# Decode block with sliding-window attention and a feed-forward: the loads' buffers as one tile, and three weight matrices in two loads each

## The chip, the cores and the metric

The kernel runs on one core of a Trainium2 chip, as one launch. The metric is the device time of one execution in microseconds (us), given as the median of several runs. The profile is of one execution taken by the hardware profiler. Engines: TensorE (PE, with PEld for its weight loads), VectorE (DVE), ScalarE (ACT), GpSimd (POOL) and SyncE (SP), which issues every DMA of this kernel.

## The reference

All values are float32. B = 2 tokens, D = 512, 32 query heads over 8 key/value heads of 128, a window of the last 4096 positions of a cache of 32768, and a feed-forward of F = 1792.

```python
mod = silu(c) @ w_mod                       # [2, 6*512]: sa, ca, ga, sb, cb, gb
h = layernorm(x) * (1 + ca) + sa
q = h @ wq                                  # [2, 32*128]
o = softmax(q . k_window / sqrt(128)) @ v_window
x = x + ga * (o @ wo)
h = layernorm(x) * (1 + cb) + sb
x = x + gb * (silu(h @ w1) @ w2)
```

Bytes read: w_mod 6.3 MB, wq 8.4 MB, keys and values 67.1 MB, wo 8.4 MB, w1 and w2 3.7 MB each.

## The kernel before

All weights, keys and values stream through a ring of 8 buffers of 16 KB per partition (pool `ring`, L55; `stream`, L69). Each load takes the next buffer, so load number i can be issued when the work that reads load i - 8 is done. SP issues the loads in one order: w_mod in 4 loads of 128 rows (`load_rows`, L72), then wq in 4 (L112), then by `fetch` (L324) keys and values of the 8 heads and 2 tokens, 32 loads of 2 MB, then wo in 4 loads of 8 rows per partition (`load_runs`, L91, called at L473), w1 in 3 and w2 in 5. In `load_rows` partition p holds row 128k + p of load k; in `load_runs` partition p holds neighbouring rows of the matrix, one contiguous run.

The two tokens lie on few partitions. A vector of 512 is held in one of two ways: the "ch" form (c_ch, x_ch; L100, four DMAs with runs of 128 bytes, L105 to L110) fits contraction in blocks of 128 rows, and the "spread" form (x_sp, L474, one DMA with runs of 512 bytes) puts 128 neighbouring values on one partition. `turned` (L268) transposes a spread tile so that partition p, column k is element 4p + k.

Steps: c is transposed (cT, L235), silu is taken, and w_mod gives m_ch (sa, ca in "ch" form, L246) and m_sp (the other four, spread, L249). Layernorm a (`moments`, L209) and mod_ch give h_a, transposed to hq_T (L263). Then 64 instructions for q (L285) and a rearrangement to qbd.

The loop over heads (L448) is software-pipelined: `keys` transposes K on VectorE (kT, L337), `scores` on TensorE (L349), `maxima`, `exponentials` on ScalarE, `turn` and `weighted` (o, L423) for the head before. `inorder` keeps the program's order on an engine.

After the last head come the sums and the normalised output oTn (oq L512, L515). Output projection: for q = 0 to 23 a matmul of 512 columns with rows of wo (acc_o, L550), four column groups in turn; for q = 24 to 31 four matmuls of 128 columns each (ao, L561); `gather` (L519) copies acc_o on ScalarE and folds it into ao with four matmuls after q = 27. `busy(n)` (L534) runs n matmuls on a junk tile whose result is not used (L537): busy(5) after q = 15 and after q = 23, busy(2) after the last. A float32 matmul is two instructions in the trace.

Then aoT (L572), x1T, the mean (L582), hT_b, and w1's matmuls (hid, L595) for k = 0 to 3, with the variance (L606) after k = 1 and busy(2) after k = 2. hidT (L615), silu, uT (L627), w2's matmuls: tt = 0 to 7 wide (acc_yw, L631), tt = 8 to 13 in four pieces (acc_y, L643) with a gather after tt = 10, then yo (L653, L654) and the store (L656).

```python
    for q in range(24):
        g = q % 4
        inorder(nc.tensor.matmul(acc[32 * g : 32 * g + 32, :], oTn[:, q, :],
            wot[q // 8][:, q % 8, :], start=(q < 4), stop=(q >= 20)))
        if q in (15, 23):
            busy(5)
```

Of the kernel before, what the change touches and what calls it, by code (L numbers as in the profile page):

```python
# [23 lines left out]
def adaln_block(  # L24
# [23 lines left out]

    head = ctx.enter_context(tc.tile_pool(name="head", bufs=1))
    id4 = head.tile([P, 32], F32, name="id4")
    ring = ctx.enter_context(tc.tile_pool(name="ring", bufs=RING))  # L55
# [7 lines left out]
    def const(shape, name):  # L63
        return consts.tile(shape, F32, name=name)

    def bank(tag, name):
        return (psum1 if tag in "CO" else psum).tile([P, 512], F32, tag=tag, name=name)

    def stream(name):  # L69
        return ring.tile([P, 4096], F32, tag="st", name=name)  # L70

    def load_rows(name, w, k, width):  # L72
        t = stream(f"{name}{k}")[:, :width]
        nc.sync.dma_start(t, w[k * P : (k + 1) * P, :])
        return t

    def load_k(b, h):
        t = stream(f"k{h}_{b}")
        nc.sync.dma_start(
            t, k_cache[b, h, SK - W :, :].rearrange("(p n) d -> p (n d)", p=P)  # L80
        )
        return t

    def load_v(b, h):
        t = stream(f"v{h}_{b}")
        nc.sync.dma_start(
            t, v_cache[b, h, SK - W :, :].rearrange("(p n) d -> p (n d)", p=P)
        )
        return t

    def load_runs(name, w, per, lo, hi):  # L91

        e = w.shape[1]
        t = stream(f"{name}{lo}")[:, : (hi - lo) * e].rearrange("p (q e) -> p q e", e=e)
        nc.sync.dma_start(t, w.rearrange("(p q) e -> p q e", q=per)[:, lo:hi, :])
        return t


    x2 = x.rearrange("b s d -> (b s) d")
    x_sp, x_ch, c_ch = const([P, P], "x_sp"), const([P, P], "x_ch"), const([P, P], "c_ch")  # L100
    for t in (c_ch, x_ch, x_sp):
        nc.vector.memset(t, 0.0)
    wm = [load_rows("wm", w_mod, 0, 6 * D)]
    rows8 = lambda t: t.rearrange("(ab r) m -> ab r m", r=16)[:, 0, :]
    for t, src in ((c_ch, c), (x_ch, x2)):  # L105
        for b in range(B):
            nc.sync.dma_start(
                rows8(t)[b : 2 * 4 : 2, :].rearrange("a (k c) -> a k c", k=4),
                src[b, :].rearrange("(k a c) -> a k c", k=4, a=4),
            )  # L110
    wm += [load_rows("wm", w_mod, k, 6 * D) for k in range(1, 4)]
    wqt = [load_rows("wq", wq, k, HQ * DH) for k in range(4)]  # L112
# [80 lines left out]

    oTn = const([P, 32, 32], "oTn")
    nc.gpsimd.memset(oTn, 0.0)
    mod_ch = const([P, 2, P], "mod_ch")
    mod_sp = const([P, 4, P], "mod_sp")
    x1 = const([P, P], "x1")

# [31 lines left out]
        return mean, rstd  # L231


    cT = const([P, 4, 32], "cT")
    nc.vector.transpose(cT.rearrange("p k r -> p (k r)"), c_ch)  # L235
    sg = silu_exp(cT, "sgc", [P, 4, 32])
    scT = const([P, 4, 32], "scT")
    nc.vector.tensor_mul(scT, cT, sg)
    m_ch = bank("A", "m_ch")[:, : 2 * P]
    m_sp = bank("D", "m_sp")  # L240
    for k in range(4):
        ab = wm[k][:, : 2 * D].rearrange("p (s k a c) -> p a s k c", s=2, k=4, a=4)
        cd = wm[k][:, 2 * D :].rearrange("p (s g m) -> p g s m", s=4, g=4)
        for g in range(4):
            r = slice(32 * g, 32 * g + 32)
            nc.tensor.matmul(m_ch[r, :], scT[:, k, :], ab[:, g], start=(k == 0), stop=(k == 3))  # L246
        for g in range(4):
            r = slice(32 * g, 32 * g + 32)
            nc.tensor.matmul(m_sp[r, :], scT[:, k, :], cd[:, g], start=(k == 0), stop=(k == 3))  # L249
        if k == 0:  # L250
            mean_a, rstd_a = moments(x_ch, "a")
            xn = once.tile([P, P], F32, tag="xp", name="xn_a")
            nc.vector.tensor_scalar(
                xn, x_ch, mean_a, rstd_a, op0=ALU.subtract, op1=ALU.mult
            )

    nc.vector.tensor_copy(mod_ch[:, 0, :], m_ch[:, :P])
    nc.vector.tensor_scalar(mod_ch[:, 1, :], m_ch[:, P:], 1.0, None, op0=ALU.add)
    h_a = once.tile([P, P], F32, tag="pr", name="h_a")
    nc.vector.tensor_mul(h_a, xn, mod_ch[:, 1, :])  # L260
    nc.vector.tensor_add(h_a, h_a, mod_ch[:, 0, :])
# [6 lines left out]
    def turned(t, name):  # L268
        o = const([P, 4, 32], name)
        nc.vector.transpose(o, t.rearrange("p (m k) -> p k m", k=4))  # L270
        return o
# [9 lines left out]
    for k in range(4):  # L281
        wv = wqt[k].rearrange("p (n s g m) -> p n g s m", n=2, s=4, g=G)
        for n in range(2):
            for g in range(G):
# [4 lines left out]
                    start=(k == 0),  # L289
                    stop=(k == 3),  # L290
                )
    for n in range(2):
        qT = once.tile([P, D], F32, tag="wide", name=f"qT{n}").rearrange("p (s j r) -> p s j r", s=4, r=32)
        nc.vector.transpose(qT.rearrange("p s j r -> p (s j r)"), q_ps[n])  # L294
        for g in range(G):
            r = slice(32 * g, 32 * g + 32)
# [8 lines left out]
        for i in range(4):  # L305
            r = slice(32 * i, 32 * i + 32)
# [14 lines left out]
    kt, vt, wot, kT = {}, {}, [], {}  # L321
# [173 lines left out]
    for r in (0, 64):  # L495
# [4 lines left out]
            start=True,  # L500
            stop=True,
# [32 lines left out]
    def busy(n):  # L534

        for _ in range(n):
            inorder(nc.tensor.matmul(  # L537
                junk[0:32, :256],
                id4,
                selh.rearrange("p m y -> p (m y)")[:, :256],  # L540
                start=True,
                stop=True,
            ))
# [4 lines left out]
    for q in range(24):  # L548
        g = q % 4
        inorder(nc.tensor.matmul(  # L550
            acc[32 * g : 32 * g + 32, :],
            oTn[:, q, :],
            wot[q // 8][:, q % 8, :],
            start=(q < 4),
            stop=(q >= 20),
        ))
        if q in (15, 23):
            busy(5)
    for q in range(24, 32):
        for g in range(4):  # L560
            inorder(nc.tensor.matmul(  # L561
                ao[32 * g : 32 * g + 32, :],
                oTn[:, q, :],
                wot[3][:, q - 24, g * P : (g + 1) * P],
                start=(q == 24),
                stop=(q == 31),
            ))
# [4 lines left out]
    nc.vector.transpose(aoT, ao.rearrange("p (m k) -> p k m", k=4))  # L572
    x1T = once.tile([P, 4, B], F32, tag="x1T", name="x1T")
# [19 lines left out]
    for k in range(4):  # L593
        for g in range(4):
            inorder(nc.tensor.matmul(  # L595
                hp[32 * g : 32 * g + 32, :],
                hT[:, k, :],
                w1t[k][:, g * FC : (g + 1) * FC],
                start=(k == 0),
                stop=(k == 3),  # L600
            ))
# [15 lines left out]
    for b in range(B):  # L617
# [5 lines left out]
            op0=ALU.mult,  # L623
            op1=ALU.add,
# [4 lines left out]
    for tt in range(WIDE):  # L629
        g = tt % 4  # L630
# [4 lines left out]
            start=(tt < 4),  # L635
            stop=(tt >= WIDE - 4),
# [4 lines left out]
    for tt in range(WIDE, T2):  # L641
        for g in range(4):
# [4 lines left out]
                start=(tt == WIDE),  # L647
                stop=(tt == T2 - 1),
# [35 lines left out]
```

## Time and profile before

| | before |
|---|---|
| median of 3 runs | 236.98 us (236.98 to 237.25) |
| the profiled execution | 236.89 us |
| its span, first to last instruction | 235.0 us |
| mean granted TensorE clock | 0.869 |
| PE / PEld / DVE / ACT / POOL busy | 146.5 / 45.9 / 114.6 / 25.4 / 10.3 us |
| moved by DMA | 97.69 MB, mean 416 GB/s |

The span is the time from the first to the last instruction; the execution's time has a little more around it. Busy times of engines overlap. The slices of the page cut the span in 40 equal parts; a digit is a busy share in tenths. PEclk is the share of TensorE's full clock that was granted. In a timeline row stand the start, the time, the engine, the line, the operation, what it writes and reads, the number of instructions and, in brackets, the idle time of the engine before them with what ended it.

### The profile page before, as it was taken

How to read it: one execution, taken by the hardware profiler on the slowest of the kernel's cores; microseconds unless marked ns; L12 is line 12 of the kernel's file. 1: busy time of each engine (PE TensorE's matmuls, PEld its weight loads, DVE VectorE, ACT ScalarE, POOL GpSimd, SP SyncE). 2: the span in 40 equal slices, each digit the busy share in tenths (PEclk: the TensorE clock that was granted, in tenths of full speed). 3: DMA queues.
4: the chain of work that ended last, by engine and by line, in shares of the span. 5: the costliest groups of instructions: out<-in, count | busy, mean ns of one | idle time of the engine just before them, and what ended most of it. 6: DMA issues, size and time to landing. Idle time of an engine off the chain costs nothing.

```text
span 235.0 us, 2644 instructions
## 1 busy us (share of the span) xinstructions
PE 146.5 (62%) x1094; PEld 45.9 (20%) x1094; DVE 114.6 (49%) x176; ACT 25.4 (11%) x56; POOL 10.3 (4%) x30
## 2 busy tenths in 40 slices
PE   0086546367187577667549519626743967788993
PEld 0032101101011121121112102111211222335332
DVE  0634000793694792693892792595298050002130
ACT  2200000100300200200200200200020021003210
POOL 8600000100000000000000000000000000000000
PEclk9999975759869997999976967965985799999999
DMA  6999999999999999999999999999999999999991
GB/s 253 426 438 427 427 438 427 424 439 427 429 441 424 427 438 427 429 438 424 429 435 429 427 432 432 432 429 432 428 429 429 429 432 429 432 426 422 421 412 56
DMA packets 7603, 97.69 MB, mean 416 GB/s; under 512 B 920, under 2 KB 936, under 8 KB 1576
## 3 DMA queue, kind: packets, MB, share of 16 engines
q1 hardware_dynamic: 7592, 97.54, 97.5%
q8 instruction: 8, 0.13, 0.2%
q14 instruction: 3, 0.02, 0.0%
HBM read 97.53 MB, written 0.00 MB: 415 GB/s over the span
## 4 chain that ended last, share of the span: by engine, by line
DMA 64%; DVE 22%; PE 10%; ACT 2%; issue 1%; SPq 1%; DVEq 0%
DVE kT L337 16%; DMA wo<-in_A_wo_dram 14%; DMA k<-in_A_k_cache_dram 14%; DMA v<-in_A_v_cache_dram 13%; DMA wq<-in_A_wq_dram 13%; DMA w<-in_B_w_dram 7%; PE s L349 5%; DMA wm<-in_w_mod_dram 3%; DVE zp L395 2%; PE o L423 2%; PE q L285 1%; DVE xp L393 1%; ACT pr L381 1%; DVE mx L359 1%; ACT L381 1%
## 5 line engine op out<-in xcount | busy, mean ns | idle before, releaser
L337 DVE STREAM_TRANSPOSE kT<-k 128x1024 f32<-128x1024 f32 x64 | 73.7, 1210 | 1.6 <-DMA k<-in_A_k_cache_dram 1.6
L349 PE MATMUL s<-kT,qbd 128*32 128x512 f32 x256 | 44.5, 670 | 11.2 <-DVE kT L337 11.1
L423 PE MATMUL o<-v,ptb 128*32 128x512 f32 x256 | 38.5, 730 | 19.8 <-DMA v<-in_A_v_cache_dram 19.3
L359 DVE TENSOR_REDUCE mx<-s 128x1 f32<-128x512 f32 x8 | 5.5, 691 | 40.1 <-PE s L349 40.1
L349 PEld LDWEIGHTS s<-kT,qbd 128*32 128x32 f32 x256 | 11.1, 126 | 45.8 <-issue 24.1
L285 PE MATMUL q<-wq,hq_T 128*32 128x512 f32 x64 | 11.2, 836 | 10.1 <-DMA wq<-in_A_wq_dram 10.1
L423 PEld LDWEIGHTS o<-v,ptb 128*32 128x32 f32 x256 | 8.1, 124 | 35.8 <-issue 33.1
L402 PE MATMUL pT<-zp,id 128*32 128x256 f32 x64 | 5.6, 418 | 13.9 <-DVE zp L395 13.9
L379 ACT COPY bias<-bp 128x1 f32<-128x1 f32 x8 | 1.3, 159 | 111.9 <-PE bp L377 111.9
L537 PE MATMUL junk<-selh,id 128*32 128x256 f32 x46 | 11.3, 380 | 0.0
L294 DVE STREAM_TRANSPOSE qT<-q 128x512 f32<-128x512 f32 x2 | 1.4, 718 | 18.6 <-PE q L285 18.3
L395 DVE TENSOR_TENSOR zp<-xp,group 128x1024 f32<-128x1024 f32 x8 | 9.8, 1225 | 0.2
L393 DVE STREAM_TRANSPOSE xp<-pr 128x512 f32<-128x512 f32 x8 | 5.6, 701 | 4.4 <-ACT pr L381 4.4
L217 PE MATMUL mean_a<-mv_a,avg 128*128 128x1 f32 x2 | 0.6, 362 | 10.6 <-DVE mv_a L214 10.6
L361 PE MATMUL mT<-ident,mx 128*1 128x128 f32 x16 | 3.0, 270 | 6.4 <-DVE mx L359 6.4
L550 PE MATMUL acc_o<-wo,oTn 128*32 128x512 f32 x48 | 5.8, 598 | 1.9 <-DMA wo<-in_A_wo_dram 1.6
L537 PEld LDWEIGHTS junk<-selh,id 128*32 128x32 f32 x46 | 5.0, 110 | 6.7 <-issue 3.5
L438 PE MATMUL o_all<-ob,selh 128*64 128x128 f32 x64 | 5.7, 304 | 0.8 <-ACT ob L432 0.8
L270 DVE STREAM_TRANSPOSE xT<-x_sp 128x128 f32<-128x128 f32 x1 | 0.4, 403 | 11.8 <-DMA x_sp<-in_A_x_dram 11.8
L432 ACT COPY ob<-o 128x512 f32<-128x512 f32 x8 | 4.7, 585 | 10.3 <-PE o L423 10.3
L285 PEld LDWEIGHTS q<-wq,hq_T 128*32 128x32 f32 x64 | 2.1, 128 | 18.8 <-DMA wq<-in_A_wq_dram 12.5
L249 PE MATMUL m_sp<-wm,scT 128*32 128x512 f32 x32 | 5.7, 796 | 0.0
(132 smaller groups left out, 95.0 us busy)
## 6 DMA issues: line engine op xcount, KB each, us to landing
k<-in_A_k_cache_dram SPq DMA_DIRECT2D x16, 2048.0 KB, 30.2
v<-in_A_v_cache_dram SPq DMA_DIRECT2D x16, 2048.0 KB, 31.5
wq<-in_A_wq_dram SPq DMA_DIRECT2D x4, 2048.0 KB
wo<-in_A_wo_dram SPq DMA_DIRECT2D x4, 2048.0 KB, 32.3
wm<-in_w_mod_dram SPq DMA_DIRECT2D x4, 1536.0 KB, 10.2
w<-in_B_w_dram SPq DMA_DIRECT2D x2, 1024.0 KB, 23.2
w<-in_B_w_dram SPq DMA_DIRECT2D x1, 1792.0 KB
w<-in_B_w_dram SPq DMA_DIRECT2D x2, 896.0 KB
```

The costliest lines, as they stand in the source:

```text
L249: nc.tensor.matmul(m_sp[r, :], scT[:, k, :], cd[:, g], start=(k == 0), stop=(k == 3))
L285: nc.tensor.matmul(q_ps[n][32 * g : 32 * g + 32, :], hq_T[:, k, :], wv[:, n, g], start=(k == 0), stop=(k == 3),)
L337: inorder(nc.vector.transpose(kT[h, b][:, :, 8 * n4 : 8 * n4 + 8, :].rearrange("p j n k -> p n j k"), kt[h, b][:, n4 * 1024 : (n4 + 1) * 1 ...
L349: inorder(nc.tensor.matmul(s_ps[h][r : r + 32, :], qbd[h // 4][:, h % 4, b, j, :], kT[h, b][:, j, 16 * c : 16 * c + 16, :], start=(j == 0) ...
L359: inorder(nc.vector.tensor_reduce(mx, s_ps[h], axis=AX.X, op=ALU.max))
L393: inorder(nc.vector.transpose(xp, pr[h]))
L395: inorder(nc.vector.tensor_mul(zp, xp[:, None, :, 0:16].to_broadcast([P, 4, 16, 16]), group[:, :, None, None].to_broadcast([P, 4, 16, 16]),))
L402: inorder(nc.tensor.matmul(tp[32 * i : 32 * i + 32, :], id4, zp.rearrange("p a s x -> p (a s) x")[:, :, 4 * i : 4 * i + 4], start=True, st ...
L423: inorder(nc.tensor.matmul(o_ps[h][32 * c : 32 * c + 32, :], ptb[h % 2][:, 256 * b + 32 * w : 256 * b + 32 * w + 32], vt[h, b][:, 512 * w ...
L438: inorder(nc.tensor.matmul(o_all[r : r + 64, :], selh[:, m, HQ - G - G * h : 3 * HQ - G - G * h], o_sb[h][:, m * DH : (m + 1) * DH], start ...
L537: inorder(nc.tensor.matmul(junk[0:32, :256], id4, selh.rearrange("p m y -> p (m y)")[:, :256], start=True, stop=True,))
L550: inorder(nc.tensor.matmul(acc[32 * g : 32 * g + 32, :], oTn[:, q, :], wot[q // 8][:, q % 8, :], start=(q < 4), stop=(q >= 20),))
```

## The change

- The ring becomes one tile of 8 slots; `stream(n)` gives the next n slots, starting at a multiple of n. A load of up to 4096 floats per partition takes one slot, a larger one two.
- w_mod, wq and wo are loaded by `load_runs` in two loads each, of 24576 (w_mod) or 32768 bytes per partition; w1 in two loads of 14336 bytes instead of three.
- The "ch" form goes: c and x are loaded spread, one DMA each; x_sp is loaded at the start and no longer ahead of w1. The transposes use `turned`. The number and shapes of the matmuls of these steps stay.
- busy after the wo matmuls: busy(15) after q = 15 instead of busy(5) after q = 15 and q = 23. busy(4) after the variance (k = 1) instead of busy(2) after k = 2.
- The five w2 loads stand after the wo matmuls in the program.

```diff
-    ring = ctx.enter_context(tc.tile_pool(name="ring", bufs=RING))
+    ring = ctx.enter_context(tc.tile_pool(name="ring", bufs=1))
...
-    def stream(name):
-        return ring.tile([P, 4096], F32, tag="st", name=name)
-
-    def load_rows(name, w, k, width):
-        t = stream(f"{name}{k}")[:, :width]
-        nc.sync.dma_start(t, w[k * P : (k + 1) * P, :])
-        return t
+
+    slots, turn_of = ring.tile([P, RING, 4096], F32, name="slots"), [0]
+
+    def stream(n=1):
+        i = turn_of[0]
+        i += -i % n
+        turn_of[0] = i + n
+        return slots[:, i % RING : i % RING + n, :].rearrange("p s e -> p (s e)")
...
-    def load_runs(name, w, per, lo, hi):
+    def load_runs(w, per, lo, hi):
 
         e = w.shape[1]
-        t = stream(f"{name}{lo}")[:, : (hi - lo) * e].rearrange("p (q e) -> p q e", e=e)
+        n = 1 if (hi - lo) * e <= 4096 else 2
+        t = stream(n)[:, : (hi - lo) * e].rearrange("p (q e) -> p q e", e=e)
         nc.sync.dma_start(t, w.rearrange("(p q) e -> p q e", q=per)[:, lo:hi, :])
         return t
...
-    wm = [load_rows("wm", w_mod, 0, 6 * D)]
+    halves = lambda t: [t[:, 0, :], t[:, 1, :]]
+    wm = halves(load_runs(w_mod, 4, 0, 2))
     rows8 = lambda t: t.rearrange("(ab r) m -> ab r m", r=16)[:, 0, :]
-    for t, src in ((c_ch, c), (x_ch, x2)):
-        for b in range(B):
-            nc.sync.dma_start(
-                rows8(t)[b : 2 * 4 : 2, :].rearrange("a (k c) -> a k c", k=4),
-                src[b, :].rearrange("(k a c) -> a k c", k=4, a=4),
-            )
-    wm += [load_rows("wm", w_mod, k, 6 * D) for k in range(1, 4)]
-    wqt = [load_rows("wq", wq, k, HQ * DH) for k in range(4)]
+    for t, src in ((c_sp, c), (x_sp, x2)):
+        nc.sync.dma_start(rows8(t), src.rearrange("b (g m) -> g b m", m=P))
+    wm += halves(load_runs(w_mod, 4, 2, 4))
+    wqt = halves(load_runs(wq, 4, 0, 2)) + halves(load_runs(wq, 4, 2, 4))
...
-    cT = const([P, 4, 32], "cT")
-    nc.vector.transpose(cT.rearrange("p k r -> p (k r)"), c_ch)
+    cT = turned(c_sp, "cT")
...
-        ab = wm[k][:, : 2 * D].rearrange("p (s k a c) -> p a s k c", s=2, k=4, a=4)
+        ab = wm[k][:, : 2 * D].rearrange("p (s g m) -> p g s m", s=2, g=4)
...
-    hq_T = const([P, 4, 32], "hq_T")
-    nc.vector.transpose(hq_T.rearrange("p k r -> p (k r)"), h_a)
+    hq_T = turned(h_a, "hq_T")
...
-    for q0 in range(0, 32, 8):
-        wot.append(load_runs("wo", wo, 32, q0, q0 + 8))
-    nc.sync.dma_start(rows8(x_sp), x2.rearrange("b (g m) -> g b m", m=P))
+    for q0 in (0, 16):
+        wot.append(load_runs(wo, 32, q0, q0 + 16))
     xT = turned(x_sp, "xT")
     w1t = []
-    for lo, hi in ((0, 2), (2, 3), (3, 4)):
-        wt = load_runs("w1_", w1, 4, lo, hi)
+    for lo, hi in ((0, 2), (2, 4)):
+        wt = load_runs(w1, 4, lo, hi)
         w1t.extend(wt[:, k, :] for k in range(hi - lo))
-    T2, WIDE = F // P, 8
-    w2t = {}
-    for lo, hi in ((0, 4), (4, WIDE), (WIDE, 11), (11, 13), (13, T2)):
-        wt = load_runs("w2_", w2, T2, lo, hi)
-        for tt in range(lo, hi):
-            w2t[tt] = wt[:, tt - lo, :]
...
-            wot[q // 8][:, q % 8, :],
+            wot[q // 16][:, q % 16, :],
...
-        if q in (15, 23):
-            busy(5)
+        if q == 15:
+            busy(15)
...
-                wot[3][:, q - 24, g * P : (g + 1) * P],
+                wot[1][:, q - 16, g * P : (g + 1) * P],
...
     busy(2)
+    T2, WIDE = F // P, 8
+    w2t = {}
+    for lo, hi in ((0, 4), (4, WIDE), (WIDE, 11), (11, 13), (13, T2)):
+        wt = load_runs(w2, T2, lo, hi)
+        for tt in range(lo, hi):
+            w2t[tt] = wt[:, tt - lo, :]
...
-        if k == 2:
-            busy(2)
...
             nc.vector.reciprocal(rstd, std)
+            busy(4)
     busy(5)
```

More of the change, by code (lines that the diff above doesn't have):

```diff
@@ L67, in bank @@
         return (psum1 if tag in "CO" else psum).tile([P, 512], F32, tag=tag, name=name)
-    def stream(name):
-        return ring.tile([P, 4096], F32, tag="st", name=name)
-    def load_rows(name, w, k, width):
-        t = stream(f"{name}{k}")[:, :width]
-        nc.sync.dma_start(t, w[k * P : (k + 1) * P, :])
-        return t
+    slots, turn_of = ring.tile([P, RING, 4096], F32, name="slots"), [0]
[4 more added lines that the diff above has]
+        return slots[:, i % RING : i % RING + n, :].rearrange("p s e -> p (s e)")
     def load_k(b, h):
-        t = stream(f"k{h}_{b}")
+        t = stream()
         nc.sync.dma_start(
@@ L84, in load_v @@
     def load_v(b, h):
-        t = stream(f"v{h}_{b}")
+        t = stream()
         nc.sync.dma_start(
@@ L99, in adaln_block @@
     x2 = x.rearrange("b s d -> (b s) d")
-    x_sp, x_ch, c_ch = const([P, P], "x_sp"), const([P, P], "x_ch"), const([P, P], "c_ch")
-    for t in (c_ch, x_ch, x_sp):
+    x_sp, c_sp = const([P, P], "x_sp"), const([P, P], "c_sp")
+    for t in (c_sp, x_sp):
         nc.vector.memset(t, 0.0)
-    wm = [load_rows("wm", w_mod, 0, 6 * D)]
+    halves = lambda t: [t[:, 0, :], t[:, 1, :]]
+    wm = halves(load_runs(w_mod, 4, 0, 2))
     rows8 = lambda t: t.rearrange("(ab r) m -> ab r m", r=16)[:, 0, :]
-    for t, src in ((c_ch, c), (x_ch, x2)):
-        for b in range(B):
-            nc.sync.dma_start(
-                rows8(t)[b : 2 * 4 : 2, :].rearrange("a (k c) -> a k c", k=4),
-                src[b, :].rearrange("(k a c) -> a k c", k=4, a=4),
-            )
-    wm += [load_rows("wm", w_mod, k, 6 * D) for k in range(1, 4)]
-    wqt = [load_rows("wq", wq, k, HQ * DH) for k in range(4)]
+    for t, src in ((c_sp, c), (x_sp, x2)):
+        nc.sync.dma_start(rows8(t), src.rearrange("b (g m) -> g b m", m=P))
+    wm += halves(load_runs(w_mod, 4, 2, 4))
+    wqt = halves(load_runs(wq, 4, 0, 2)) + halves(load_runs(wq, 4, 2, 4))
     ident = const([P, P], "ident")
@@ L195, in adaln_block @@
     nc.gpsimd.memset(oTn, 0.0)
-    mod_ch = const([P, 2, P], "mod_ch")
+    mod_a = const([P, 2, P], "mod_a")
     mod_sp = const([P, 4, P], "mod_sp")
@@ L231, in moments, with turned @@
         return mean, rstd
-    cT = const([P, 4, 32], "cT")
-    nc.vector.transpose(cT.rearrange("p k r -> p (k r)"), c_ch)
+    def turned(t, name):
+        o = const([P, 4, 32], name)
+        nc.vector.transpose(o, t.rearrange("p (m k) -> p k m", k=4))
+        return o
+    cT = turned(c_sp, "cT")
     sg = silu_exp(cT, "sgc", [P, 4, 32])
@@ L238, in adaln_block @@
     nc.vector.tensor_mul(scT, cT, sg)
-    m_ch = bank("A", "m_ch")[:, : 2 * P]
+    m_a = bank("A", "m_a")[:, : 2 * P]
     m_sp = bank("D", "m_sp")
     for k in range(4):
-        ab = wm[k][:, : 2 * D].rearrange("p (s k a c) -> p a s k c", s=2, k=4, a=4)
+        ab = wm[k][:, : 2 * D].rearrange("p (s g m) -> p g s m", s=2, g=4)
         cd = wm[k][:, 2 * D :].rearrange("p (s g m) -> p g s m", s=4, g=4)
@@ L245, in adaln_block @@
             r = slice(32 * g, 32 * g + 32)
-            nc.tensor.matmul(m_ch[r, :], scT[:, k, :], ab[:, g], start=(k == 0), stop=(k == 3))
+            nc.tensor.matmul(m_a[r, :], scT[:, k, :], ab[:, g], start=(k == 0), stop=(k == 3))
         for g in range(4):
@@ L250, in adaln_block @@
         if k == 0:
-            mean_a, rstd_a = moments(x_ch, "a")
+            mean_a, rstd_a = moments(x_sp, "a")
             xn = once.tile([P, P], F32, tag="xp", name="xn_a")
             nc.vector.tensor_scalar(
-                xn, x_ch, mean_a, rstd_a, op0=ALU.subtract, op1=ALU.mult
+                xn, x_sp, mean_a, rstd_a, op0=ALU.subtract, op1=ALU.mult
             )
-    nc.vector.tensor_copy(mod_ch[:, 0, :], m_ch[:, :P])
-    nc.vector.tensor_scalar(mod_ch[:, 1, :], m_ch[:, P:], 1.0, None, op0=ALU.add)
+    nc.vector.tensor_copy(mod_a[:, 0, :], m_a[:, :P])
+    nc.vector.tensor_scalar(mod_a[:, 1, :], m_a[:, P:], 1.0, None, op0=ALU.add)
     h_a = once.tile([P, P], F32, tag="pr", name="h_a")
-    nc.vector.tensor_mul(h_a, xn, mod_ch[:, 1, :])
-    nc.vector.tensor_add(h_a, h_a, mod_ch[:, 0, :])
-    hq_T = const([P, 4, 32], "hq_T")
-    nc.vector.transpose(hq_T.rearrange("p k r -> p (k r)"), h_a)
+    nc.vector.tensor_mul(h_a, xn, mod_a[:, 1, :])
+    nc.vector.tensor_add(h_a, h_a, mod_a[:, 0, :])
+    hq_T = turned(h_a, "hq_T")
     nc.scalar.copy(mod_sp.rearrange("p s m -> p (s m)"), m_sp)
@@ L266, in adaln_block @@
     ga, sb, cb1, gb = (mod_sp[:, s, :] for s in range(4))
[L268 to L271, printed above, removed]
     hT, uT = const([P, 4, 32], "hT_b"), const([P, F // P, 32], "uT")
```

## The prediction

> **What bounds the kernel now.** I read the page from the top: the slices of part 2, the DMA issues of part 6, then the timeline of the last 35 us and a table of the TensorE clock in stretches of 3.41 us.
>
> ```profile
> span 235.0 us, 2644 instructions
> ...
> PE 146.5 (62%) x1094; PEld 45.9 (20%) x1094; DVE 114.6 (49%) x176; ACT 25.4 (11%) x56; POOL 10.3 (4%) x30
> ...
> PEclk9999975759869997999976967965985799999999
> DMA  6999999999999999999999999999999999999991
> GB/s 253 426 438 427 427 438 427 424 439 427 429 441 424 427 438 427 429 438 424 429 435 429 427 432 432 432 429 432 428 429 429 429 432 429 432 426 422 421 412 56
> ...
> k<-in_A_k_cache_dram SPq DMA_DIRECT2D x16, 2048.0 KB, 30.2
> ```
>
> A slice is 5.9 us. The DMA row stands at 9 in all slices but the first and the last: one stream of loads runs from start to end at 424 to 441 GB/s. A load is issued about 30 us before it lands (last figure of the issue rows), so six loads of 4.9 us are always queued. A compute step that comes some us later does not starve this stream; only the end, after the last loads, and the stream's own pace set the time. So the tail must be read instruction by instruction. The next rows are TensorE's; the first number is the start, the second the time of the group, the bracket is the idle time before a group and who ended it, and "x16" counts instructions, two for each matmul of the code.
>
> ```profile
> 200.11 1.08 PE L512 MATMUL oq<-on,quad 128*128 128x64 f32 x8 [0.80 <-DVE on L509]
> 201.55 1.92 PE L550 MATMUL acc_o<-wo,oTn 128*32 128x512 f32 x16 [0.36 <-DVE oTn L515]
> 204.20 1.93 PE L550 MATMUL acc_o<-wo,oTn 128*32 128x512 f32 x16 [0.73 <-DMA wo<-in_A_wo_dram]
> 205.94 2.32 PE L537 MATMUL junk<-selh,id 128*32 128x256 f32 x10
> 209.10 1.93 PE L550 MATMUL acc_o<-wo,oTn 128*32 128x512 f32 x16 [0.84 <-DMA wo<-in_A_wo_dram]
> ...
> 213.95 1.08 PE L561 MATMUL ao<-wo,oTn 128*32 128x128 f32 x32 [0.79 <-DMA wo<-in_A_wo_dram]
> 214.85 0.40 PE L524 MATMUL ao<-acc_o_sb,id 128*32 128x128 f32 x8
> ...
> 218.28 1.71 PE L595 MATMUL hid<-w,hT_b 128*32 128x448 f32 x16
> ...
> 220.33 0.96 PE L595 MATMUL hid<-w,hT_b 128*32 128x448 f32 x8
> ...
> 222.52 0.96 PE L595 MATMUL hid<-w,hT_b 128*32 128x448 f32 x8 [0.39 <-DMA w<-in_B_w_dram]
> ...
> 225.98 1.06 PE L631 MATMUL acc_yw<-w,uT 128*32 128x512 f32 x8 [0.36 <-DVE uT L627]
> ...
> 228.32 1.03 PE L537 MATMUL junk<-selh,id 128*32 128x256 f32 x4
> 229.36 0.86 PE L643 MATMUL acc_y<-w,uT 128*32 128x128 f32 x24
> 230.01 0.43 PE L524 MATMUL acc_y<-acc_y_sb,id 128*32 128x128 f32 x8
> 230.53 1.06 PE L643 MATMUL acc_y<-w,uT 128*32 128x128 f32 x24
> ```
>
> The same stretch on ScalarE and VectorE, four steps of the chain between those matmuls:
>
> ```profile
> 211.45 0.58 ACT L522 COPY acc_o_sb<-acc_o 128x512 f32<-128x512 f32 x1 [12.85 <-PE acc_o L550]
> ...
> 216.19 0.32 DVE L572 STREAM_TRANSPOSE aoT<-ao 128x128 f32<-128x128 f32 x1 [2.50 <-PE ao L561]
> ...
> 223.55 0.65 DVE L615 STREAM_TRANSPOSE hidT<-hid 128x448 f32<-128x448 f32 x1 [2.74 <-PE hid L595]
> ...
> 231.66 0.29 DVE L653 TENSOR_TENSOR yo<-acc_y,mod_sp 128x128 f32<-128x128 f32 x1 [5.73 <-PE acc_y L643]
> ```
>
> See how the four wo loads are eaten as they land: the second at 204.20, the third at 209.10, the fourth at 213.95, 4.90 and 4.85 us apart. Each brings 16 instructions of 1.93 us, and junk matmuls (busy) fill the rest. When the last wo load lands, only the ao matmuls remain. The same holds for w1: the last quarter lands at 222.52 and has 8 instructions behind it. The work behind each landing is small, which is why the end follows the stream: yo at 231.66, 0.6 us after the last matmuls got their w2.
>
> **The change, part by part.** *Fewer, larger loads.* Seven of the 52 large loads go: two of wm, two of wq, two of wo, one of w1. The trace holds no load of 24 or 32 KB per partition. Its nearest rows: 2 MB loads run at about 430 GB/s (4.87 us each), the mix of w1 and w2 loads (some 1.1 MB on average) at 421 to 422, or 2.72 us each. Two unknowns, two equations: 442 GB/s and 0.12 us per load if all of the difference were a cost per load; nothing if it were not. I take 0.05 us, in the middle, since sizes and patterns differ too. Five of the seven merges lie ahead of the first wo landing: 0.25 us; seven: 0.35 us. That is what the stream gains. The other end of the bound is 0.6 us for five; a loss of the same size I can't exclude, as larger packets were never run.
>
> *The start.* The conditioning vector now queues behind 3 MB instead of 1.5 MB, so cT comes some 3.7 us later (1.5 MB at 426 GB/s), and wq's last half brings 32 instructions instead of 16 after its landing.
>
> ```profile
> 39.01 3.33 PE L285 MATMUL q<-wq,hq_T 128*32 128x512 f32 x16 [2.06 <-DMA wq<-in_A_wq_dram]
> ...
> 45.95 4.62 DVE L337 STREAM_TRANSPOSE kT<-k 128x1024 f32<-128x1024 f32 x4
> ...
> 48.38 1.91 PE L349 MATMUL s<-kT,qbd 128*32 128x512 f32 x2 [3.38 <-DVE kT L337]
> ```
>
> 16 more at the slow rate of the first row are 3.3 us, at the fast rate 1.9: the keys start at 48 to 49 instead of 45.95. The cover is the 30 us queue of loads and VectorE, idle half of its time (49% busy): a head's loads take 19.5 us, so the lag is made up within a head or two. I cost the start at nothing; without the cover it would be 2 to 3 us. The spread form does the same number of matmuls on the same shapes, and four loads of 2 KB and a late one of 4 KB become two: nothing.
>
> *wo in two loads.* This one is on the path. The first half lands with the old second load, 204.20 less 0.25 = 203.95. Then 16 of the code's matmuls run (32 instructions; 1.74 us per 16, from 204.20 to the junk at 205.94): 3.48 us. Then busy(15), 30 instructions: from 2.32 us for ten and 1.03 for four, 0.215 each, 6.45 us. At full clock that ends at 213.88. The second half lands at 213.95 - 0.30 = 213.65, so even at full clock there is no reserve. And TensorE now idles from 201.19, the end of oq, to 203.95, as the first wo work no longer fills that gap. What that does is seen in the clock table (columns: stretch, length, PE, PEld, DVE, ACT, POOL busy, PEclk, DMA share, GB/s):
>
> ```profile
> 24.85:28.26 3.41, 0.58 (x12) 0.22 (x12) 0.00 (x0) 0.00 (x0) 0.00 (x0) 1.00 1.00 428
> 28.27:31.68 3.41, 2.67 (x16) 0.29 (x8) 0.00 (x0) 0.00 (x0) 0.00 (x0) 0.50 1.05 447
> 31.68:35.09 3.41, 0.93 (x12) 0.33 (x16) 0.00 (x0) 0.00 (x0) 0.00 (x0) 1.00 0.97 413
> 35.09:38.50 3.41, 1.86 (x12) 0.12 (x4) 0.00 (x0) 0.00 (x0) 0.00 (x0) 0.50 1.00 428
> 38.50:41.91 3.41, 2.90 (x16) 0.59 (x16) 0.86 (x2) 0.00 (x0) 0.03 (x1) 0.50 1.03 442
> 52.16:55.57 3.41, 1.73 (x7) 0.29 (x10) 2.92 (x3) 0.00 (x0) 0.00 (x0) 1.00 1.03 442
> 55.57:58.98 3.41, 3.19 (x26) 0.74 (x18) 0.19 (x1) 0.00 (x0) 0.00 (x0) 1.00 1.02 437
> 171.62:175.03 3.41, 1.53 (x20) 0.60 (x16) 3.38 (x4) 0.96 (x2) 0.00 (x0) 1.00 1.00 428
> 175.04:178.45 3.41, 0.00 (x0) 0.00 (x0) 3.41 (x4) 0.00 (x0) 0.00 (x0) 0.50 1.01 432
> 198.93:202.34 3.41, 2.25 (x24) 1.39 (x24) 0.88 (x3) 0.00 (x0) 0.00 (x0) 1.00 1.02 437
> ```
>
> The clock changes only at these borders, which repeat every 3.41 us. A stretch at full clock with 0.58, 0.93 or 1.53 us of matmul is followed by one at 0.50; 1.73 keeps it. From 0.50, 1.86 was not enough, 2.67 was. Before, the stretch 198.93 to 202.34 held 2.25. Without acc_o (0.79 of it) it holds 1.46: half clock from 202.34. The next holds 205.75 - 203.95 = 1.8: still half, until 209.17. That is 5.2 us at half clock, 2.6 us lost. The borders need not fall there in another execution. A border at 203.5 costs 1.5 us (2.96 of work in the next stretch, so one stretch only), at 204.6 1.7 us (a whole stretch at half). Sliding the border, every place gives a fall of the clock, and the loss goes from 1.2 to 2.8 with a mean of 1.9, which I take.
>
> The Trainium skill, page "TensorE: Matmul & The Clock Gate", Part 1, says that the clock falls after at least one idle window of about 3.4 us. By that rule the gap of 2.8 us would cost nothing; the first stretch above disagrees, as it held 0.58 us of work, no idle longer than 2.83 us, and was followed by 0.50. That rule's outcome is the second rival below.
>
> The tail now: q16 starts at 213.88 + 1.9 = 215.8. Its eight matmuls, formerly done before the last landing, take 1.74, so ao can start at 217.5 and acc_o ends at 217.7. ScalarE copies acc_o (0.58; it began 0.4 after the end of the matmuls at 211.03 before, and I allow 0.2): the gather starts at 218.5. From gather to aoT 1.34 as before: 219.85. aoT to hid 2.09: 221.95. The first half of w1 has landed; hid k=0, 1 and var take 2.05 (218.28 to 220.33): 224.0. busy(4) replaces busy(2) and sits ahead of k=2, 8 x 0.215 = 1.72: 225.7. Then k=2 and 3, 1.71: 227.4; w1's second half landed at about 222.2, so its merge costs nothing of its own. hidT at 227.5, yw 2.43 later at 229.95. From there nothing waits for w2 (the last group began at 230.53, with its last wait for w2 inside it, so all has landed by 231): 2.34 to the junk, 0.86 of junk, 0.65, 0.2 for the gather, 0.9 for the last group: 4.9, where 5.68 with waits stood before. yo at 234.85, against 231.66: **3.2 us later**. The store after it is unchanged.
>
> *w2's issue moves behind the wo matmuls.* Loads 0 to 7 take buffers of the last values and go out as before. The next two need the first wo half's 16 matmuls (done about 209), the last needs the second half's (about 219.9). On SP only the output store is queued behind them. At 209 the stream still owes the rest of wo, w1 and half of w2, some 18 us; at 219.9 it owes 10. Nothing is late; if the cover were gone, a load of 256 KB issued at 219.9 would still land before 229.95 + 4.
>
> **The sum.** The profiled execution took 236.89 us (span 235.0), 0.09 under the median of 236.98; 236.89 + 3.2 = 240.1.
>
> **Rivals.** *The clock holds* (the rule of the idle window): the 1.9 goes, 238.2. For it: before, this stage stayed at 1.00 throughout. Against it: every stretch with under 1.6 us of work was followed by half clock, those around the first matmuls of the kernel aside. *The stream gains more and is the bound again, faster than before.* Its place is the third wq load:
>
> ```profile
> 27.74 3.19 PE L285 MATMUL q<-wq,hq_T 128*32 128x512 f32 x16 [2.83 <-DMA wq<-in_A_wq_dram]
> 34.16 2.79 PE L285 MATMUL q<-wq,hq_T 128*32 128x512 f32 x16 [3.22 <-DMA wq<-in_A_wq_dram]
> ```
>
> It landed 6.42 us after the second, where 4.85 is normal. If the larger loads avoid such a slip, all later landings come 1.57 earlier. This decides only from a landing of the first wo half that is over 1.3 us earlier and with the clock held or nearly so: 238.2 - 1.57 = 236.6; with the upper per-load cost (0.4 more), 236.2. With the clock down it is 238.5. Against it: nothing ties the slip to the size of a load. *The loads wait for each other*, as all buffers are one tile: the change would undo the queue. Some 44 landings with about 1.6 us from issue to first data (first issue at 0.7, and 253 against 430 GB/s in the first slice) add 70 us: 310. Against it: kT is one tile written by four transposes, and the scores at 48.38 began after two of them, so waits go by the part that is touched.
>
> **How the numbers follow.** Forecast 0.72 (239.4 to 241.0 from the clock's bounds); clock held 0.12 (238.2); stream 0.13, of which 0.08 faster and 0.05 within 0.2%; waits 0.03. A measurement of this kernel tells 0.2%, about 0.5 us, from no change. So slower 0.87, same 0.05, faster 0.08. The range takes in the forecast, its stream bounds of 0.3 either way, and the held clock: 237.9 to 241.3; left out are the stream's cases, the waits and a rest.
>
> **What would show it.** Right: PEclk near 0.5 somewhere between 202 and 209; a PE gap of about 2.8 us ahead of acc_o; q16 starting over 1 us after its load's landing, with no DMA wait in its bracket; hidT near 227.5; no DMA wait at the last acc_y; DMA slices unchanged until 229. Wrong: acc_o's 32 instructions in 3.5 us; a first wo landing earlier than 203; acc_y still waiting for w2; DMA slices below 9.

## The result, and the profile after

The changed kernel takes 240.47 us (median of 6 runs, 239.52 to 240.86) against 237.02 before: 1.0135 of the time before, interval 1.0121 to 1.0149. It is 3.4 us slower by the medians, 3.2 us by the ratio. The profiled execution took 240.82 us.

The page of the changed kernel, the lines that answer to those of before:

```profile
span 238.7 us, 2656 instructions
...
PE 150.8 (63%) x1108; PEld 49.0 (21%) x1108; DVE 114.0 (48%) x175; ACT 25.4 (11%) x56; POOL 10.4 (4%) x30
...
PEclk9999587955959997999999979957965999599999
DMA  7999999999999999999999999999999999999940
GB/s 264 450 430 439 439 431 395 439 428 426 431 430 434 434 423 426 439 431 431 434 426 428 431 431 434 426 431 434 431 434 428 423 445 441 428 416 423 418 189 1
```

The stream is as full as before, and as fast but for one slice (395 in the seventh, 427 before). What is new is its end: the last slice but one is half empty and the last quite, where only the last was. And PEclk shows a 5 near the end (slice 35, 203 to 209 us). The stream's end in stretches of one microsecond (columns as in the clock table of the prediction):

```profile
228.00:229.00 1.00, 1.00 (x6) 0.51 (x5) 0.65 (x1) 0.00 (x0) 0.00 (x0) 1.00 0.91 367
229.00:230.00 1.00, 1.00 (x6) 0.48 (x5) 0.67 (x4) 0.23 (x1) 0.00 (x0) 1.00 0.58 227
230.00:231.00 1.00, 0.65 (x6) 0.16 (x8) 0.61 (x3) 0.00 (x0) 0.00 (x0) 1.00 0.09 35
231.00:232.00 1.00, 1.00 (x13) 0.37 (x9) 0.00 (x0) 0.00 (x0) 0.00 (x0) 1.00 0.00 0
```

The last load has landed before 231, and TensorE has only just begun w2's matmuls (acc_yw, 230.74). TensorE's rows of the tail, with the lines of the changed kernel (acc_o is L537, ao L548, hid L588):

```profile
200.04 1.08 PE L499 MATMUL oq<-on,quad 128*128 128x64 f32 x8 [0.80 <-DVE on L496]
204.19 6.04 PE L537 MATMUL acc_o<-slots,oTn 128*32 128x512 f32 x32 [3.07 <-DMA slots<-in_A_wo_dram]
210.04 6.42 PE L524 MATMUL junk<-selh,id 128*32 128x256 f32 x29
216.09 0.63 PE L537 MATMUL acc_o<-slots,oTn 128*32 128x512 f32 x3
...
216.52 1.88 PE L537 MATMUL acc_o<-slots,oTn 128*32 128x512 f32 x13
217.84 1.44 PE L548 MATMUL ao<-slots,oTn 128*32 128x128 f32 x32
219.49 0.43 PE L511 MATMUL ao<-acc_o_sb,id 128*32 128x128 f32 x8 [0.22 <-ACT acc_o_sb L509]
...
222.86 1.71 PE L588 MATMUL hid<-slots,hT_b 128*32 128x448 f32 x16
...
226.13 0.58 PE L588 MATMUL hid<-slots,hT_b 128*32 128x448 f32 x3
...
230.74 1.07 PE L623 MATMUL acc_yw<-slots,uT 128*32 128x512 f32 x8 [0.35 <-DVE uT L619]
```

After the first wo landing no bracket names a DMA any more: TensorE itself is late. Its 16 code matmuls on the first half of wo take 5.85 us (204.19 to 210.04), where 1.74 per eight at full clock would be 3.48. The junk then runs to 216.1; the second half of wo, which the runs below show landing at about 213.8, waits for it. On VectorE and ScalarE the steps in between:

```profile
218.85 0.58 ACT L509 COPY acc_o_sb<-acc_o 128x512 f32<-128x512 f32 x1 [20.32 <-PE acc_o L537]
...
220.86 0.32 DVE L565 STREAM_TRANSPOSE aoT<-ao 128x128 f32<-128x128 f32 x1 [19.43 <-PE ao L548]
...
228.31 0.65 DVE L607 STREAM_TRANSPOSE hidT<-hid 128x448 f32<-128x448 f32 x1 [2.94 <-PE hid L588]
...
235.56 0.29 DVE L645 TENSOR_TENSOR yo<-acc_y,mod_sp 128x128 f32<-128x128 f32 x1 [4.87 <-PE acc_y L635]
```

yo is at 235.56, 3.90 later than before. The clock in stretches of 3.41 us, borders where this execution had them:

```profile
198.84:202.25 3.41, 1.48 (x16) 1.12 (x12) 0.88 (x3) 0.00 (x0) 0.00 (x0) 1.00 1.06 454
202.25:205.66 3.41, 1.47 (x8) 0.46 (x12) 0.00 (x0) 0.00 (x0) 0.00 (x0) 0.50 0.94 404
205.67:209.08 3.41, 3.41 (x20) 0.90 (x16) 0.00 (x0) 0.00 (x0) 0.00 (x0) 0.50 0.91 389
209.08:212.49 3.41, 3.41 (x24) 1.53 (x17) 0.00 (x0) 0.00 (x0) 0.00 (x0) 1.00 1.00 427
```

The stretch with the gap holds 1.48 us of matmul and the clock falls; the next holds 1.47 and it stays down for a whole further stretch, although TensorE is busy in all of it.

### The profile page after: what moved, and what is told of

It reads as the page before. It is cut to its first block, busy times and chain, and to the rows that moved or that the text cites. A ratio compares the mean times of both kernels' runs of the same rounds, so it can differ in the third digit from the quotient of the medians.

```text
span 238.7 us, 2656 instructions
## 1 busy us (share of the span) xinstructions
PE 150.8 (63%) x1108; PEld 49.0 (21%) x1108; DVE 114.0 (48%) x175; ACT 25.4 (11%) x56; POOL 10.4 (4%) x30
## 4 chain that ended last, share of the span: by engine, by line
DMA 42%; PE 26%; DVE 26%; ACT 3%; issue 2%; SPq 1%; POOL 1%; POOLq 0%; ACTq 0%
DVE kT L332 17%; DMA slots<-in_A_wq_dram 15%; DMA slots<-in_A_v_cache_dram 14%; DMA slots<-in_A_wo_dram 13%; PE s L344 9%; PE junk L524 4%; PE acc_o L537 3%; PE o L418 2%; DVE zp L390 2%; PE q L280 2%; DVE mx L354 1%; PE hid L588 1%; ACT pr L376 1%; DVE xp L388 1%; PE acc_yw L623 1%
## 5 line engine op out<-in xcount | busy, mean ns | idle before, releaser
L332 DVE STREAM_TRANSPOSE kT<-slots 128x1024 f32<-128x1024 f32 x64 | 73.7, 1210 | 1.7 <-DMA slots<-in_A_k_cache_dram 1.7
L344 PE MATMUL s<-kT,qbd 128*32 128x512 f32 x256 | 47.7, 672 | 12.6 <-DVE kT L332 12.6
L418 PE MATMUL o<-slots,ptb 128*32 128x512 f32 x256 | 37.0, 706 | 14.6 <-DMA slots<-in_A_v_cache_dram 14.1
L280 PE MATMUL q<-slots,hq_T 128*32 128x512 f32 x64 | 10.7, 828 | 11.5 <-DMA slots<-in_A_wq_dram 11.5
L524 PE MATMUL junk<-selh,id 128*32 128x256 f32 x60 | 14.1, 380 | 0.0
L418 PEld LDWEIGHTS o<-slots,ptb 128*32 128x32 f32 x256 | 7.8, 121 | 29.9 <-issue 27.1
L537 PE MATMUL acc_o<-slots,oTn 128*32 128x512 f32 x48 | 8.3, 814 | 3.1 <-DMA slots<-in_A_wo_dram 3.1
L524 PEld LDWEIGHTS junk<-selh,id 128*32 128x32 f32 x60 | 6.4, 110 | 7.3 <-issue 2.1
L280 PEld LDWEIGHTS q<-slots,hq_T 128*32 128x32 f32 x64 | 2.6, 146 | 19.7 <-issue 13.4
L372 PE MATMUL bp<-negscale,mrow 1*128 1x1 f32 x16 | 3.0, 255 | 4.2 <-DVE mrow L365 4.2
```

Of the source, the lines that this page charges most:

```text
L280: nc.tensor.matmul(q_ps[n][32 * g : 32 * g + 32, :], hq_T[:, k, :], wv[:, n, g], start=(k == 0), stop=(k == 3),)
L332: inorder(nc.vector.transpose(kT[h, b][:, :, 8 * n4 : 8 * n4 + 8, :].rearrange("p j n k -> p n j k"), kt[h, b][:, n4 * 1024 : (n4 + 1) * 1 ...
L344: inorder(nc.tensor.matmul(s_ps[h][r : r + 32, :], qbd[h // 4][:, h % 4, b, j, :], kT[h, b][:, j, 16 * c : 16 * c + 16, :], start=(j == 0) ...
L418: inorder(nc.tensor.matmul(o_ps[h][32 * c : 32 * c + 32, :], ptb[h % 2][:, 256 * b + 32 * w : 256 * b + 32 * w + 32], vt[h, b][:, 512 * w ...
L524: inorder(nc.tensor.matmul(junk[0:32, :256], id4, selh.rearrange("p m y -> p (m y)")[:, :256], start=True, stop=True,))
```

## The experiments

The theory to test: the loss is TensorE's work between and behind the two wo landings (the clock, the junk, the matmuls moved behind the landing), the tail theory. Rivals: the larger loads or the later start cost the time (stream theory); the clock does not follow from this gap. Each time is a median beside runs of the kernel before on the same chip, with the ratio to it and its 95% interval; the baseline was 236.95 us for the first four, 237.09 for the next four, 236.94 for the last two. What a run gains on the changed kernel is given by the medians. By the ratios, which tell the changed kernel to some 0.3 us, the gains of the second, third and fourth run are 2.2, 2.3 and 1.4 us instead of 2.4, 2.6 and 1.6.

**wo back in four loads**, all else as changed.

```diff
-    for q0 in (0, 16):
-        wot.append(load_runs(wo, 32, q0, q0 + 16))
+    for q0 in range(0, 32, 8):
+        wot.append(load_runs(wo, 32, q0, q0 + 8))
...
-        if q == 15:
-            busy(15)
+        if q in (15, 23):
+            busy(5)
```

> The changed kernel with wo alone put back: four loads, busy(5) after q = 15 and after q = 23. Tail theory (the loss is TensorE's work behind the two wo landings: half clock after the gap 1.2 to 2.8 us, the rest the matmuls now behind the last landing): acc_o runs at full clock, the end follows the stream again, 236.5 to 237.2 us. Stream theory (the loss comes from the larger loads or the later start): still 239 to 240, as w_mod, wq and w1 keep their larger loads. w1's merge and busy(4) should cost under 0.3 us here, hidden by the wait for w2.

Measured: 236.69 us, 0.999 (0.998 to 0.9999). The whole loss is gone with this one part. Its TensorE rows:

```profile
200.55 5.33 PE L537 MATMUL acc_o<-slots,oTn 128*32 128x512 f32 x32 [0.36 <-DVE oTn L502]
205.71 2.32 PE L524 MATMUL junk<-selh,id 128*32 128x256 f32 x10
208.87 1.92 PE L537 MATMUL acc_o<-slots,oTn 128*32 128x512 f32 x16 [0.84 <-DMA slots<-in_A_wo_dram]
210.61 2.32 PE L524 MATMUL junk<-selh,id 128*32 128x256 f32 x10
213.73 1.08 PE L548 MATMUL ao<-slots,oTn 128*32 128x128 f32 x32 [0.80 <-DMA slots<-in_A_wo_dram]
...
222.19 1.71 PE L588 MATMUL hid<-slots,hT_b 128*32 128x448 f32 x16 [0.30 <-DMA slots<-in_B_w_dram]
```

The last two wo landings end waits again, at 208.87 and 213.73, and so does w1's second half at 222.19. The last weight loads of acc_y wait 0.2 us for w2, at 230.83, and yo follows 0.5 us later, as before (231.16 and 231.66): the end follows the stream again. The expectation that acc_o runs at full clock was wrong in this execution: its first 32 instructions took 5.2 us, and PEclk stood at 0.5 from 200.6 to 204.0. It cost nothing, since busy(5) still ended before the next landing. That is a first hint that the fall of the clock is not the whole story.

**Six junk matmuls in the gap**, ahead of acc_o, nothing else.

```diff
+    busy(6)
     for q in range(24):
```

> The changed kernel with six junk matmuls (12 instructions, 2.6 us) in the gap between oq and the first wo landing; nothing else moved. Tail theory: the clock stays at 1.00, the first 32 acc_o instructions take 3.5 us instead of 5.85, q = 16 starts at 214.1 instead of 216.5, 238.2 us. If the clock does not follow from this gap, or the stream is the cause: 240.2 to 240.8, no change.

Measured: 238.03 us, 1.0043 (1.0028 to 1.0058), 2.4 us less than the changed kernel.

```profile
199.71 4.42 PE L524 MATMUL junk<-selh,id 128*32 128x256 f32 x12
204.09 3.64 PE L538 MATMUL acc_o<-slots,oTn 128*32 128x512 f32 x32
207.52 6.42 PE L524 MATMUL junk<-selh,id 128*32 128x256 f32 x29
213.77 0.62 PE L538 MATMUL acc_o<-slots,oTn 128*32 128x512 f32 x1
```

The clock of that stretch, in windows of 2 us (columns as in the clock table of the prediction):

```profile
200.00:202.00 2.00, 2.00 (x6) 0.87 (x5) 0.08 (x1) 0.00 (x0) 0.00 (x0) 0.50 0.99 426
202.00:204.00 2.00, 2.00 (x8) 0.70 (x6) 0.00 (x0) 0.00 (x0) 0.00 (x0) 0.73 0.91 393
```

acc_o takes 3.43 us to the junk's start, as worked out. But the clock did not stay at 1.00: it fell at 199.7, with the first junk, and the twelve instructions took 4.42 us instead of 2.6. They filled the slow stretch, and at 203.1 the clock was back, ahead of the landing. Adding work made the kernel faster, so what TensorE does in the gap decides the clock at which acc_o runs.

**busy(8) instead of busy(15)**, the gap as it is.

```diff
-            busy(15)
+            busy(8)
```

> The changed kernel with busy(8) instead of busy(15): 14 junk instructions fewer, 3.0 us. The gap and the fall of the clock stay. Tail theory: TensorE is free at 213.5, just ahead of the second wo landing at 213.7, so 2.6 us are saved: 237.8. Stream theory: no change, 240.2 to 240.8.

Measured: 237.85 us, 1.0037 (1.0024 to 1.0050), 2.6 us less.

```profile
204.23 5.90 PE L537 MATMUL acc_o<-slots,oTn 128*32 128x512 f32 x32 [3.18 <-DMA slots<-in_A_wo_dram]
209.94 3.62 PE L524 MATMUL junk<-selh,id 128*32 128x256 f32 x16
213.90 1.92 PE L537 MATMUL acc_o<-slots,oTn 128*32 128x512 f32 x16 [0.34 <-DMA slots<-in_A_wo_dram]
```

Here acc_o runs at half clock until 208.8, nearly as in the changed kernel, and takes 5.71 us, and yet the result is that of the filled gap. The second wo half lands at about 213.8 and TensorE waits for it by 0.3 us.

**No busy(4)** between the variance and w1's k = 2.

```diff
             nc.vector.reciprocal(rstd, std)
-            busy(4)
```

> The changed kernel without busy(4) between the variance and w1's k = 2: 8 junk instructions fewer. Tail theory: these 1.72 us lie on the path, as w1's second half landed long before: 238.7. Stream theory, or if something else than TensorE is late there: no change, 240.2 to 240.8.

Measured: 238.85 us, 1.0077 (1.0062 to 1.0092), 1.6 us less, where 1.72 was worked out: k = 2 follows the variance at once.

```profile
222.50 1.71 PE L588 MATMUL hid<-slots,hT_b 128*32 128x448 f32 x16
224.14 0.38 PE L597 MATMUL var_b<-vs,mean 128*128 128x2 f32 x2
224.45 1.71 PE L588 MATMUL hid<-slots,hT_b 128*32 128x448 f32 x16
```

**All three edits** at once, with busy(13) as the shorter filler.

```diff
+    busy(6)
     for q in range(24):
...
-            busy(15)
+            busy(13)
...
-            busy(4)
```

> The changed kernel with three edits at once: busy(6) in the gap ahead of acc_o, busy(13) instead of busy(15), no busy(4). Tail theory: q = 16 starts at its landing (213.8), acc_y waits for w2 again as before, 236.5 to 236.9 us: the eight wo matmuls behind the landing and w1's merge alone (2.5 us) are then absorbed by the tail's slack. If these are worth more than the slack, 237.2 to 238.0.

Measured: 236.47 us, 0.9975 (0.9967 to 0.9984): 0.6 us faster than the kernel before. wo stays in two loads, with eight more matmuls behind the last landing, and w1 in two; the tail absorbs these.

```profile
213.81 1.92 PE L538 MATMUL acc_o<-slots,oTn 128*32 128x512 f32 x16 [0.45 <-DMA slots<-in_A_wo_dram]
```

q = 16 starts at its landing and acc_y waits for w2 again, both as expected. But that last wait is only 0.16 us (the weight loads at 230.80), so the tail has hardly any slack left over.

**The first merges undone too**: wo, w_mod and wq in four loads each.

```diff
-    wm = halves(load_runs(w_mod, 4, 0, 2))
+    one = lambda w, k: load_runs(w, 4, k, k + 1)[:, 0, :]
+    wm = [one(w_mod, 0)]
...
-    wm += halves(load_runs(w_mod, 4, 2, 4))
-    wqt = halves(load_runs(wq, 4, 0, 2)) + halves(load_runs(wq, 4, 2, 4))
+    wm += [one(w_mod, k) for k in range(1, 4)]
+    wqt = [one(wq, k) for k in range(4)]
```

> The kernel with wo in four loads (e1) with w_mod and wq in four loads as well, so that of the merges only w1's stays. If a merged load saves 0.05 us: last w2 landing 0.2 us later than in e1 and 236.9 us; if larger loads gain nothing: 236.7; if they cost, 236.5. The keys then start at 46 instead of 48 us: if that lag counted, over 1 us would be gained.

Measured: 237.09 us, 1.0001 (0.9992 to 1.0010). Against the run with wo alone in four (0.999) this is 0.26 us more, on intervals of 0.1% each, which together are as wide as the difference: that the four merges gain the 0.2 us worked out is likely and not shown, but they cost nothing that these runs can tell. Undoing the later start of the keys (first scores at 48.60) gained nothing either. In the two profiled executions the later wo landings lie 0.6 us apart (208.87 and 213.73 against the rows below); how much of that belongs to the merges and how much to one execution is left open.

```profile
209.47 1.93 PE L537 MATMUL acc_o<-slots,oTn 128*32 128x512 f32 x16 [0.86 <-DMA slots<-in_A_wo_dram]
211.21 2.32 PE L524 MATMUL junk<-selh,id 128*32 128x256 f32 x10
214.32 1.08 PE L548 MATMUL ao<-slots,oTn 128*32 128x128 f32 x32 [0.79 <-DMA slots<-in_A_wo_dram]
```

**How much work the gap needs**: the second experiment with busy(3), and with busy(1).

```diff
-    busy(6)
+    busy(3)
     for q in range(24):
```

> The changed kernel with three junk matmuls (1.29 us) in the gap ahead of acc_o, placed right behind oq. By the rule read from the stretches (under some 1.6 us of matmul in a stretch of 3.41 us and the clock falls), the rest of the gap, 1.7 us, is short enough at every place of the border as the gap before is short too: 238.0 as with six. If the whole gap had to be filled: 239 or more.

> The changed kernel with one junk matmul (0.43 us) in the gap. By the same rule the clock still falls at nearly every place of the border: 239.3 to 240.8, mean 240.2. If any work in the gap is enough (the gap's longest idle time counts, 2.5 us here): 238.0.

Measured: busy(3) 238.09 us, 1.0051 (1.0030 to 1.0072), the same as six; one of its eight runs, at 240.10, looks like a fall of the clock that the rule did not foresee; it has no profile. busy(1) 241.01 us, 1.0161 (1.0143 to 1.0179): no gain, as foreseen, but 0.2 above the end of the expected range; its profiled execution had the first wo landing 0.5 later (acc_o at 204.72), why is open. First the profile of busy(3), then that of busy(1):

```profile
199.81 2.77 PE L524 MATMUL junk<-selh,id 128*32 128x256 f32 x6
204.21 3.64 PE L538 MATMUL acc_o<-slots,oTn 128*32 128x512 f32 x32 [1.63 <-DMA slots<-in_A_wo_dram]
```

```profile
204.72 5.04 PE L538 MATMUL acc_o<-slots,oTn 128*32 128x512 f32 x32 [3.15 <-DMA slots<-in_A_wo_dram]
209.58 6.42 PE L524 MATMUL junk<-selh,id 128*32 128x256 f32 x29
```

In the first, the clock had fallen at the junk itself (2.77 us for six instructions, 1.5 at full clock), and the junk at half speed filled enough of the stretch to bring it back before the landing; 1.63 us stayed idle without harm.

**The clock left to fall, the junk shortened**: busy(8) and no busy(4), the gap unfilled.

> The changed kernel with busy(8) instead of busy(15) and no busy(4); the gap stays unfilled, so the clock falls. If the fall costs only because junk had already used up the time between the two wo landings: TensorE is free at 213.5, ahead of the landing, and the end follows the stream as with the gap filled, 236.4 to 236.9. If the fall has a price of its own: 237.5 to 239.

Measured: 236.32 us, 0.9974 (0.9964 to 0.9983), the same as with the gap filled.

```profile
204.22 6.00 PE L537 MATMUL acc_o<-slots,oTn 128*32 128x512 f32 x32 [3.11 <-DMA slots<-in_A_wo_dram]
210.03 3.62 PE L524 MATMUL junk<-selh,id 128*32 128x256 f32 x16
213.90 1.92 PE L537 MATMUL acc_o<-slots,oTn 128*32 128x512 f32 x16 [0.25 <-DMA slots<-in_A_wo_dram]
```

Half clock on acc_o until 209.0, 5.81 us, and still as fast as any kernel of the study. The fall of the clock has no price of its own as long as TensorE is free when the second half of wo lands. It had one in the changed kernel because busy(15) had been laid into the 9.7 us between the two landings without reserve.

**w1 in three loads again**, all else as changed.

```diff
-    for lo, hi in ((0, 2), (2, 4)):
+    for lo, hi in ((0, 2), (2, 3), (3, 4)):
```

> The changed kernel with w1 in three loads as before; all else stays. Tail theory: w1's last piece lands at 222.3 in either case, long before busy(4) ends at 226, so nothing changes: 240.0 to 241.0. If w1's merge carries a part of the loss (its 0.86 us of matmuls behind the landing): 239.6.

Measured: 239.98 us, 1.0130 (1.0115 to 1.0145). The interval covers the changed kernel's ratio, 1.0135, but by the medians the result lies between the two expectations, so the times alone leave a part of the 0.86 us open. The traces close it: with w1 in two loads or in three, no instruction of TensorE waits for w1, so its merge carries no part of this loss.

## Why the prediction was right

**Direction and size** came out: 240.1 forecast, 240.47 measured, from the step that was named. Undoing wo's part alone gave back all of the loss. That the forecast is as near as 0.4 us is partly luck: the terms below are off by up to 0.5 us, some one way and some the other.

**The stream's gain** (0.25 us to the first wo landing, 0.35 in all): at the first wo landing it did not show; acc_o began at 204.19, against 204.20 before, and not at 203.95. At the end it did: in three runs whose end follows the loads (wo in four, all three edits, clock left to fall) the last w2 landing ends its wait at 230.80 to 230.96, against 231.16 before, 0.2 to 0.36 earlier. Two readings were off: the slices between the first and the last held 412 to 441 GB/s, not 424 to 441, and all eight w1 and w2 loads average 0.92 MB, not 1.1, which puts the upper bound at 0.08 us per load instead of 0.12. The slip of a wq load, the faster rival's place, did not vanish. The two halves of wq land 10.82 us apart, where twice 4.85 would be normal:

```profile
27.81 5.49 PE L280 MATMUL q<-slots,hq_T 128*32 128x512 f32 x32 [6.21 <-DMA slots<-in_A_wq_dram]
38.63 5.20 PE L280 MATMUL q<-slots,hq_T 128*32 128x512 f32 x32 [5.33 <-DMA slots<-in_A_wq_dram]
```

A likely cause, not tested, stands in both traces: an instruction fetch of 16 KB takes 0.92 us of DMA time at 31.6 us before and 0.96 us at 31.9 us after, and from then on the pieces of one load land 1.7 to 2.2 us apart, where they landed within 0.6 to 0.7 us.

**The start at nothing**: confirmed. The first scores ran at 50.35 instead of 48.38, and undoing that lag gained nothing.

```profile
50.35 1.91 PE L344 MATMUL s<-kT,qbd 128*32 128x512 f32 x2 [3.38 <-DVE kT L332]
```

**The clock**: 1.9 us taken as the mean over the border's places, from 1.2 to 2.8. This execution lost 5.85 - 3.48 = 2.4, and its borders fell nearly where those of the execution before had, for which 2.6 was worked out. Four runs above leave the gap empty too, and their profiled executions show the loss go by the border's place, as predicted:

| run | the clock falls at | acc_o to the junk | lost |
|---|---|---|---|
| the changed kernel | 202.25 | 5.85 us | 2.4 us |
| clock left to fall | 202.2 | 5.81 us | 2.3 us |
| busy(8) | 202.0 | 5.71 us | 2.2 us |
| no busy(4) | 201.6 | 5.56 us | 2.1 us |
| w1 in three | 200.25 | 4.96 us | 1.5 us |

Their mean is 2.1. So the scatter of the six runs, 1.3 us against 0.4 before (239.52 to 240.86, where 239.4 to 241.0 was worked out), is very likely the border's place too, though only one of the six has a profile. That the stage stood at 1.00 throughout before, which spoke for the held clock, was the luck of one execution's border: the clock fell at 200.6 with wo in four loads and at 200.1 with w_mod and wq in four as well, where nothing opens a gap.

The rule read from the stretches (under 1.6 us of matmul the clock falls, 1.73 keeps it) is too sharp. In seven of the experiments' executions the clock fell ahead of acc_o after a stretch of 1.73 to 1.85, among them the last two rows of the table. The stretches of all twelve profiled executions, those around the first matmuls aside, give this: at full clock, under 1.6 us the clock fell (one exception, 1.44), over 1.9 it held, and between them it went either way. From half clock, under 2.6 it stayed down, over 2.85 it came back, and between them either. That every place of the border gives a fall with the gap empty held in all five executions of the table.

The rule of the Trainium skill, page "TensorE: Matmul & The Clock Gate", Part 1, that the clock falls after an idle window of about 3.4 us, is not borne out here: the gap was 3.07 us, its stretch held 1.48 us of work, and the clock fell. The remark in the same part of that page of the Trainium skill, that the window runs free and the place varies from run to run, agrees with the places in the table, 200.25 to 202.25.

**The tail's terms**: the junk and busy(4) were right to a tenth or two (2.6 and 1.6 us by their own runs). Mis-sized was the wait of ScalarE's copy of acc_o: I allowed 0.2 us from the last matmul to its start, though before it had been 0.4; it began at 218.85, 0.45 after acc_o's end (216.52 + 1.88). Step by step against the forecast: the landing 0.25 late and the clock 0.45, so acc_o's end at 218.4 instead of 217.7 (its first three instructions at 216.09 ran beside the last junk, and the end came no sooner for it); the copy's start 0.25, so aoT 1.0 late; the steps after it together 0.3 shorter, so yo 0.7 late and hidT at 228.31 instead of 227.5. That is the measured 3.90 against 3.2.

**Where the reasoning was incomplete**: the prediction added the clock's fall and the junk as two terms, and only the clock could go away in its rivals. The runs show one delay: what counts is whether TensorE is free when the second wo half lands. Filling the gap (-2.4), or shortening the junk (-2.6), removes the same delay, and both together with busy(4) gone (236.47) give no more than the shortening with busy(4) gone (236.32). The junk that was there to hold the clock was what turned a slower clock into a later end.

## What to carry to other kernels

When loads are merged, the work that used to start at each landing moves behind the last one and leaves a gap ahead of the first: work out both, for the engine that eats the loads, with its clock at half. Filler matmuls between two landings need a reserve of at least what a slow clock adds, here 2.4 us; the filler is worth its place only where something on the path runs faster for it. A stream that is never empty hides a late start of 2 us, but not a late end.

## What the runs showed of the hardware that was not expected

Loads with 24 or 32 KB per partition ran as fast as those with 16 KB: in the slices that carry them the stream held 430 to 450 GB/s at the start (2 to 6) and 416 to 445 at the end (33 to 36), where the same slices before held 426 to 438; only the seventh, with the slip of wq, had 395 against 427. The clock does not need an idle stretch to fall: stretches with up to 1.88 us of matmul in 3.41 were followed by half clock. From half clock, a stretch with 1.47 us did not bring the clock back, and one with 3.41 did; 1.29 us of added junk in a 3 us gap was enough in seven runs of eight by their times, and 0.43 was not. acc_o's 32 instructions, most of them at half clock, took 5.0 to 5.9 us, where they take 3.4 to 3.5 at full clock, while the loads beside them kept their pace: the second half of wo landed 9.7 us after the first with busy(8), and 9.75 us lay between the same two landings before.
